# A 2176-token attention and two-MLP kernel: blocks of 384 and 512 tokens become one block of 128 and four of 512, and the block of 128 is multiplied with the operands' roles exchanged

## The chip, the core and the metric

One core of one Trainium2 chip. The metric is device time in microseconds (us), less is better. The kernel before was run three times: median 824.35 us, from 822.9 to 825.61.

## What is computed

The reference, cut to what matters:

```python
# attention over 4 batches x 8 heads, 512 local and 32 global tokens each, head size 64
out_g = softmax(q_g k_all^T / 8) v_all          # global queries see all 544 keys
out_l = softmax([q_l k_g^T, banded(q_l k_l^T)] / 8) [v_g, v_l]   # local: globals and 32 to each side
x = concat(out_g, out_l)                        # 2176 tokens x 512 features
for w_in, w_out in two MLPs:                    # 512 -> 2048 -> 512
    x = relu(x @ w_in) ** 2 @ w_out             # all in fp32 accuracy
```

The weights arrive as 64-bit floats and are narrowed on the chip.

## The kernel before

**Precision.** Each fp32 product of the MLPs is three matmuls in the fast fp32 form: both operands are split into a rounded part ("hi") and a remainder ("lo"), and `three` (L637 to L640) adds hi x hi, hi x lo and lo x hi in one PSUM bank. Whatever is multiplied is split first: ScalarE copies the hi part, VectorE subtracts it to make the lo part (`minus`, L271).

**Blocks.** The 2176 tokens are held with features on the partitions and tokens along the row, in five blocks: 0 (384 tokens, the last 256 local ones and the 128 global ones), 1 and 2 (512 each), 3 and 4 (384 each). Blocks 1 and 2 form pair A, blocks 3 and 4 pair B. In a matmul a 128x128 tile of the weights is the stationary operand and a block's tokens are the moving one, so a matmul of block 0 or pair B moves 384 columns and one of pair A 512.

**Stages.** The hidden layer of 2048 is worked through 256 columns at a time, 8 times in each MLP. The very first of these 16 rounds is the "first wave" (L1096 to L1103): block by block, 48 matmuls for each (24 with `first`, L784, into a bank `h`; 24 with `second`, L733, into banks `Y`). Its block 1 goes in two halves of 256. The other 15 rounds are the stages. In a stage block 0 is still worked with 48 matmuls. A pair is worked by a Winograd scheme of seven products instead of eight: `products` (L815) takes 42 matmuls, and `back` (L936) another 42. Where the table `so` says so, `plain` (L928) takes the place of `back`, with 48 matmuls a stage and less work for VectorE. The table `order` gives the sequence of A, B and 0 in each stage. The last pair of a stage is held, and its `back` is done in the next stage over both stages' products at once, so that its result is added to the running sum `y` once and not twice. Pair A goes plain in one stage's worth (stage 6), pair B in four (stage 0, two at stage 6, one at stage 7).

**What the other engines do in a stage.** For a pair: sums of products (`plus`, L869), ReLU and square (`square`, L896), four differences (`mix`, L953, on VectorE where `gt` says D), seven splits (`op`, L912: ScalarE L922, VectorE L271), fourteen additions to `y` for two stages (`deliver`, L704). For block 0: two squares, two splits, four additions to `y`, which `sd` partly gives to ScalarE as a seed of the bank (L744) and a copy back (L756). The next weights are fetched, narrowed on VectorE (L569 to L575), summed (L588) and split (L598, L271). Before each MLP `tsums` (L998) forms the input sums of both pairs: for each of two halves 8 VectorE operations (4 before the second MLP) and 4 remainders. The second square of ReLU's result goes to ScalarE or VectorE by `gf` (L907, L910).

**The attention** (`pair`, L367, 32 calls, and `glob`, L463, four calls) runs ahead of the stages, and the first wave fills TensorE's gaps in it. `glob` uses the storage of two blocks' `y` for its values (`GLOB_V`), so those blocks' first sums wait until the last `glob` is through (L688). The masks, scores and the identity matrix for transposes lie in a pool of SBUF that is given back when the attention is through; the later weight and operand buffers lie in the same space.

**Order.** Nothing is ordered by hand: each operation is given an engine, an estimated cost, a priority and its dependencies (`Plan.add`), and `Plan.order` simulates the engines and emits the program in that order. The loads go through one queue, SP's. All numbers of `CFG` (priorities such as `moe`, `glob`, `lead`, `w0`; engine choices such as `gt`, `gf`, `sx`, `xh`; buffer counts such as `NS`, `NM`, `GE`) feed that plan, so a change of them moves the order of everything.

Of the kernel before, what the change touches and what calls it, by code (L numbers as in the profile page):

```python
# [38 lines left out]
PAIRW = 1  # L39
CFG = {'warm': 13,  # L40
 'sg': 'A',
 'tl': 'DD',
 'EARLY': 4,
 'vc': 'P',
 'ev': 'AAA',
 'yc': 'AAAA',
 'wl': 'D',
 'gl': 'DD',
 'xh': 'A',
 'glob': [4.59, 16.35, 31.81, 49.0],  # L50
 'w0': 15.637277868928315,
 'w1': 0.6214172823321102,
 'halves': [1],
 'moe': [1605.016, 3061.337, 408.024, 510.431, 1148.554, 4092.57],
 'step': [0.3436, 318.4918, 0.0092, 0.0015, 18.2233, 2.7083],
 'NK': 3,
 'wa': 'AADAAAD',
 'lid': -10.973,
 'lmk': -60.126,
 'lead': 30.668,  # L60
 'vlead': 30.108,
 'NM': 2,
 'NS': 4,
 'NV': 3,
 'NR': 14,
 'NWR': 1,
# [173 lines left out]
def kernel(ctx: ExitStack, tc: tile.TileContext, kl, vl, gk, gv, gr, win, wout, msk, idn, out):  # L240
# [543 lines left out]
    def first(P, W, b, n, f, late, half=None):  # L784

        nb, c0 = (NB[b], 0) if half is None else (256, 256 * half)
        slot = W["in"][n]
        c3 = 3 * pe_r(nb)
        hk = take("h", CFG["h"] + CFG["S"] if late else CFG["h"])
        hp = bank[hk][:, 0:nb]  # L790
        for k in range(KD):
# [4 lines left out]
        if f is None:
            r, R = staging()
            square(P, nb, hp, hk, r[:, 0:nb], R)
            return r[:, 0:nb], R
# [304 lines left out]
    for layer in range(2):  # L1106
        steps = [p for p in range(STAGES) if layer or p >= FW]
        for p in steps:
# [10 lines left out]
            for n, j in enumerate(order):  # L1119
# [136 lines left out]
```

## Time and profile before

| | |
|---|---|
| median of three runs | 824.35 us |
| the profiled execution | 826.18 us |
| its span, first to last instruction | 824.1 us |
| mean granted TensorE clock | 0.990 of full speed |
| TensorE busy | 793.9 us, 6316 matmuls |
| VectorE busy | 702.4 us, 1485 instructions |
| ScalarE busy | 582.0 us, 1184 instructions |
| GpSimd busy | 61.3 us, 132 instructions |
| DMA | 188.99 MB, mean 229 GB/s |

How to read it: the time of an execution is its span and some 2 us around it. Matmuls overlap one another, so a row's duration (0.33 us for 384 columns) is longer than the time from one start to the next (0.17 us), and it is the starts that tell what a matmul costs. The same holds to a lesser degree for VectorE. A busy share is a mean over stretches with different limits; the table of stretches further down tells them apart. The granted clock has two levels here, 2.4 GHz (1.00) and half of it; a value between them is a stretch with both.

### The profile page before, as it was taken

The numbers are of one execution on the slowest core, as the hardware profiler recorded it, in microseconds if no ns is written. First come the engines' busy times: TensorE is split into PE (matmuls) and PEld (weight loads), VectorE is DVE, ScalarE is ACT, GpSimd is POOL, SyncE is SP. The second block draws the span as 40 slices with busy tenths as digits, with TensorE's granted clock in tenths as the row PEclk, the third lists the DMA queues.
The fourth block names the chain that finished last, engine by engine and source line by source line (L and its number), as shares of the span: only waits on it lengthen the run. The fifth ranks groups of instructions, "written<-read, shape, count | busy, mean of one in ns | idle before, by whom it ended". The sixth has DMA issues, their size and how long they took to land.

```text
span 824.1 us, 16763 instructions
## 1 busy us (share of the span) xinstructions
PE 793.9 (96%) x6316; PEld 701.9 (85%) x6316; DVE 702.4 (85%) x1485; ACT 582.0 (71%) x1184; POOL 61.3 (7%) x132
## 2 busy tenths in 40 slices
PE   8898899979999999999999889999999999999998
PEld 5576678978899988998899678889988998899887
DVE  4787767996989988998979996869898998999887
ACT  5795878678747774867677977778684757586853
POOL 2535254000000000000000000000000000000000
PEclk9998999989999999999999999999999999999999
DMA  9986853376729574775464479919674488557723
GB/s 342 349 317 242 305 180 103 124 269 245 281 61 346 202 281 136 258 289 207 151 238 166 166 288 319 355 39 341 247 275 138 146 331 275 181 207 285 265 82 141
DMA packets 74481, 188.99 MB, mean 229 GB/s; under 512 B 7201, under 2 KB 31905, under 8 KB 74401
## 3 DMA queue, kind: packets, MB, share of 16 engines
q1 hardware_dynamic: 74400, 187.92, 64.4%
q8 instruction: 50, 0.82, 0.4%
q14 instruction: 31, 0.25, 0.1%
HBM read 168.23 MB, written 19.66 MB: 228 GB/s over the span
## 4 chain that ended last, share of the span: by engine, by line
PE 81%; DVE 10%; DMA 4%; ACT 2%; issue 2%; SPq 1%; DVEq 0%; ACTq 0%
PE h L638 8%; PE h L640 7%; PE h L639 7%; PE O L640 6%; PE O L639 6%; PE O L638 6%; PE S L640 5%; PE S L639 5%; PE S L638 5%; PE Y L638 3%; PE Y L639 3%; PE Y L640 3%; PE PT L640 3%; PE PT L639 3%; PE PT L638 3%; PE S L393 2%
## 5 line engine op out<-in xcount | busy, mean ns | idle before, releaser
L922 ACT ACTIVATE gh<-r 128x384 fp32r<-128x384 f32 (+1 forms) x225 | 125.8, 569 | 71.3 <-PE PT L640 28.5
L271 DVE TENSOR_TENSOR gl<-r,gh 128x384 fp32r<-128x384 f32 (+2 forms) x237 | 141.2, 611 | 12.3 <-ACT gh L922 11.9
L704 DVE TENSOR_TENSOR y<-y,O 128x384 f32<-128x384 f32 (+1 forms) x115 | 68.3, 614 | 14.4 <-PE O L640 14.3
L640 PE MATMUL O<-gh,wlo 128*128 128x384 f32 (+1 forms) x208 | 74.2, 357 | 0.0
L639 PE MATMUL O<-gl,whi 128*128 128x384 f32 (+1 forms) x208 | 74.2, 357 | 0.0
L638 PE MATMUL O<-gh,whi 128*128 128x384 f32 (+1 forms) x208 | 74.1, 356 | 0.0
L910 ACT ACTIVATE r<-r 128x384 f32<-128x384 f32 (+1 forms) x131 | 72.2, 563 | 1.6
L264 POOL TENSOR_SCALAR v<-v 64x260 f32<-64x260 f32 (+2 forms) x128 | 61.1, 485 | 80.9 <-DMA v<-vl 50.7
L953 DVE TENSOR_TENSOR r<-r,r 128x512 f32<-128x512 f32 (+1 forms) x100 | 61.0, 630 | 2.5 <-ACT r L910 2.3
L271 DVE TENSOR_TENSOR wlo<-wt,whi 128x1024 fp32r<-128x1024 f32 x45 | 55.0, 1222 | 5.2 <-ACT whi L598 5.1
L598 ACT ACTIVATE whi<-wt 128x1024 fp32r<-128x1024 f32 x45 | 47.6, 1057 | 16.2 <-DVE wt L575 8.3
L638 PE MATMUL h<-xh,whi 128*128 128x384 f32 (+2 forms) x146 | 51.9, 356 | 5.7 <-ACT r L905 5.7
L903 ACT ACTIVATE r<-r 128x512 f32<-128x512 f32 (+1 forms) x75 | 43.0, 575 | 17.2 <-DVE r L869 17.1
L638 PE MATMUL h<-tr,whi 128*128 128x512 f32 (+1 forms) x138 | 52.0, 377 | 2.8 <-ACT r L256 1.6
L256 ACT ACTIVATE r<-h 128x512 f32<-128x512 f32 (+1 forms) x65 | 35.5, 546 | 25.6 <-PE h L640 25.3
L407 ACT ACTIVATE s<-s,mn 128x128 f32<-128x128 f32 x128 | 44.4, 397 | 11.4 <-DVE mn L402 10.8
L869 DVE TENSOR_TENSOR r<-r,S 128x384 f32<-128x384 f32 (+1 forms) x64 | 39.6, 623 | 14.2 <-PE S L640 11.6
L639 PE MATMUL h<-tr,whi 128*128 128x512 f32 (+1 forms) x138 | 51.7, 374 | 0.0
L640 PE MATMUL h<-tr,wlo 128*128 128x512 f32 (+1 forms) x138 | 51.6, 374 | 0.0
L588 DVE TENSOR_TENSOR wt<-wt 128x256 f32<-128x256 f32 x120 | 50.5, 421 | 1.2
L639 PE MATMUL h<-xl,whi 128*128 128x384 f32 (+2 forms) x146 | 49.2, 337 | 1.4 <-issue 1.4
L640 PE MATMUL h<-xh,wlo 128*128 128x384 f32 (+2 forms) x146 | 49.3, 338 | 0.7 <-DVE wlo L271 0.7
(174 smaller groups left out, 2234.8 us busy)
## 6 DMA issues: line engine op xcount, KB each, us to landing
tr<-tdA SPq DMA_DIRECT2D x86, 512.0 KB, 4.9
tr<-tdB SPq DMA_DIRECT2D x78, 384.0 KB, 4.5
tr<-xd SPq DMA_DIRECT2D x56, 512.0 KB, 5.1
wraw<-win SPq DMA_DIRECT2D x32, 512.0 KB, 6.1
wraw<-wout SPq DMA_DIRECT2D x32, 512.0 KB, 5.7
kq<-kl SPq DMA_DIRECT2D x32, 352.0 KB, 5.1
v<-vl SPq DMA_DIRECT2D x32, 260.0 KB, 4.8
kg<-gk SPq DMA_DIRECT2D x8, 576.0 KB, 6.8
```

Source lines behind the costliest of these rows:

```text
L264: add("Pool", 0.16 + 0.00085 * n + (0.08 if key == "nm" else 0.0), prio, lambda: nc.gpsimd.tensor_scalar(out=out_, in0=in_, scalar1=1.0 if ...
L271: add("DVE", dve(n), prio, lambda: nc.vector.tensor_tensor(out=get(out_), in0=get(a), in1=get(b), op=ALU.subtract), reads, writes, lock=True)
L407: add("Activation", 0.29, P(), lambda k=k: nc.scalar.activation(out=st[sb][:, k, :], in_=st[sb][:, k, :], func=AF.Exp, bias=mn[sb][:, k:k ...
L588: add("DVE", dve(256), P(), lambda out_=out_, a=a, b=b, op=op: nc.vector.tensor_tensor(out=half(*out_), in0=half(*a), in1=half(*b), op=op) ...
L598: nc.scalar.activation(out=whi[p], in_=tf, func=AF.Copy)
L638: nc.tensor.matmul(out=out_, lhsT=hi, rhs=xhi, start=start, stop=False, skip_group_check=again)
L639: nc.tensor.matmul(out=out_, lhsT=hi, rhs=xlo, start=False, stop=False, skip_group_check=again)
L640: nc.tensor.matmul(out=out_, lhsT=lo, rhs=xhi, start=False, stop=stop, skip_group_check=again)
L704: add("DVE", dve(nb), P(), lambda: nc.vector.tensor_tensor(out=yd, in0=yd, in1=o, op=ALU.add), (k,), (Y,))
L910: add("Activation", act(nb) + 0.04, P(), lambda: nc.scalar.activation(out=r, in_=r, func=AF.Square), (), (R,))
L922: nc.scalar.activation(out=a(), in_=r, func=AF.Copy)
L953: add("DVE", dve(nb), P(), lambda: nc.vector.tensor_tensor(out=o, in0=x, in1=z, op=ALU.subtract), rd, (O,), lock=True)
```

## The change

The blocks become 0 (the 128 global tokens), 1, 2, 3 and 4 (512 each). Pair B now moves 512 columns too. Block 0 no longer goes through `first` and `second`: in `first0` its activations are the stationary operand and the weights of both halves of the 256 hidden columns are the moving one (12 matmuls of 256 columns), so tokens land on the partitions. `second0` transposes the squared result back (2 transposes), splits it and multiplies with it as the stationary operand and 512 weight columns as the moving one (6 matmuls). The sum `y` of block 0 stays transposed, 128 tokens by 512 features, in one addition a stage, and is transposed (4 transposes) at the end of each MLP. In the first wave the last two blocks, 4 and 0, now may use the attention's banks (four in all for each kind); before only the last block did. The identity matrix moves to the lasting pool. `GLOB_V` moves from blocks 4 and 0 to 4 and 3. All of the plan's numbers are set anew; the ones spoken of here are in the diff. By the new tables pair A goes plain in one stage's worth again (6) and pair B in five (0, two at 6, one at 7, and the last, 14).

```diff
-NB = [384, 512, 512, 384, 384]
-OFF = [1792, 0, 512, 1024, 1408]
+NB = [128, 512, 512, 512, 512]
+OFF = [2048, 0, 512, 1024, 1536]
-GLOB0 = 256
-GLOB_V = (4, 0)
+GLOB0 = 0
+GLOB_V = (4, 3)
...
- 'xh': 'A',
- 'glob': [4.59, 16.35, 31.81, 49.0],
- 'w0': 15.637277868928315,
+ 'xh': 'AADD',
+ 'glob': [4.85, 15.36, 30.45, 61.1],
+ 'w0': 19.433405025148332,
...
- 'lead': 30.668,
- 'vlead': 30.108,
- 'NM': 2,
- 'NS': 4,
+ 'lead': 85.79,
+ 'vlead': 230.95,
+ 'NM': 3,
+ 'NS': 7,
...
- 'order': ['B0A', 'A0B', 'B0A', '0AB', 'B0A', '0AB', 'B0A', 'B0A', 'A0B', 'B0A', 'A0B', '0BA', 'A0B', 'B0A', 'AB0'],
+ 'order': ['B0A', 'A0B', 'BA0', 'AB0', 'B0A', '0AB', 'B0A', 'B0A', '0AB', 'BA0', '0AB', 'B0A', 'A0B', '0BA', '0AB'],
- 'gt': 'DDDDDDD',
- 'GE': 21,
- 'so': ['A', 'AB', 'B', 'A', 'AB', 'AB', '', 'A', 'A', 'B', 'AB', 'AB', 'A', 'B', 'AB'],
- 'fk': 'FKF',
- 'sx': 'D',
- 'sd': 'DADAAA',
- 'gf': 'ADAA',
+ 'gt': 'DDDDDPDD',
+ 'GE': 2,
+ 'so': ['A', 'A', 'AB', 'AB', 'B', 'AB', '', '', 'A', 'AB', 'A', 'B', 'AB', 'B', 'A'],
+ 'fk': 'FFF',
+ 'sx': 'AD',
+ 'sd': 'DAAADD',
+ 'gf': 'A',
...
-    ident = ap_.tile([128, 128], F32, name="ident")
+    ident = big.tile([128, 128], F32, name="ident")
...
+    def first0(P, W, late):
+        hk = take("h", CFG["h"] + CFG["S"] if late else CFG["h"])
+        o = bank[hk][:, 0:256].rearrange("p (f c) -> p f c", f=2)
+        for k in range(KD):
+            def go(k=k):
+                a, l = xh[0][:, k, :], xl[0][:, k, :]
+                h, r = both_(whi, W["in"])[:, k], both_(wlo, W["in"])[:, k]
+                nc.tensor.matmul(out=o, lhsT=a, rhs=h, start=k == 0, stop=False)
+                nc.tensor.matmul(out=o, lhsT=l, rhs=h, start=False, stop=False)
+                nc.tensor.matmul(out=o, lhsT=a, rhs=r, start=False, stop=k == KD - 1)
...
+        square(P, 256, bank[hk][:, 0:256], hk, r[:, 0:256], R)
+        return r, R
+    def second0(P, rR, W, stages, late, f=None):
...
+        o, tk = flip(P, r, R, 2, kinds)
...
+        split_in(P, o, tk, 256, hi, lambda: gl[f][:, 0:256], keys("gh", f, None) + lw, keys("gl", f, None), lr)
...
+        for n in range(2):
...
+                nc.tensor.matmul(out=bank[yk], lhsT=a, rhs=whi[p][:, c], start=n == 0, stop=False)
+                nc.tensor.matmul(out=bank[yk], lhsT=l, rhs=whi[p][:, c], start=False, stop=False)
+                nc.tensor.matmul(out=bank[yk], lhsT=a, rhs=wlo[p][:, c], start=False, stop=n == 1)
...
+            add("DVE", dve(512), P(), lambda: nc.vector.tensor_tensor(out=yflat[0], in0=yflat[0], in1=bank[yk], op=ALU.add), (yk,), (Y,))
+        if not end:
+            return
+        o, tk = flip(P, yflat[0], Y, 4, kinds)
...
-        last = i == len(parts) - 1
+        last = i >= len(parts) - 2
+        if b == 0:
+            second0(P, first0(P, W, last), W, (0, True, False), last, 0)
+            continue
...
-                    mine = [first(P, W, 0, i, None, True) for i in range(2)]
+                    mine = first0(P, W, True)
...
-                        second(P, 0, [op(P, NB[0], *v) for v in mine], W["out"], True, True, stages)
+                        second0(P, mine, W, stages, True)
```

## Rows read from the trace of the kernel before

**Rows 1.** Busy time, share, instructions: TensorE, its weight loads, VectorE, ScalarE, GpSimd.

```profile
PE 793.9 (96%) x6316; PEld 701.9 (85%) x6316; DVE 702.4 (85%) x1485; ACT 582.0 (71%) x1184; POOL 61.3 (7%) x132
```

**Rows 2.** Stretches: length, busy PE, PEld, DVE, ACT, POOL, granted clock, DMA, GB/s.

```profile
200.00:440.00 240.00, 240.00 (x1229) 219.85 (x1228) 215.73 (x356) 166.26 (x304) 0.00 (x0) 1.00 0.62 222
260.00:280.00 20.00, 20.00 (x107) 18.70 (x106) 19.73 (x41) 11.71 (x22) 0.00 (x0) 1.00 0.76 274
450.00:500.00 50.00, 43.73 (x208) 37.80 (x207) 49.83 (x85) 41.69 (x81) 0.00 (x0) 0.97 0.65 228
148.00:176.00 28.00, 22.48 (x113) 21.20 (x112) 27.72 (x47) 21.93 (x41) 0.00 (x0) 0.89 0.57 187
0.00:148.00 148.00, 134.45 (x2981) 101.50 (x2982) 105.36 (x491) 108.76 (x321) 61.30 (x132) 0.98 0.74 256
```

**Rows 3.** TensorE in time order, 512 columns: first and thirtieth of a run.

```profile
202.41 0.39 PE L638 MATMUL S<-xh,whi 128*128 128x512 f32 x1
...
208.98 0.39 PE L640 MATMUL PT<-gh,wlo 128*128 128x512 f32 x1
```

**Rows 4.** TensorE in time order, 384 columns: first and seventieth of a run.

```profile
419.99 0.33 PE L638 MATMUL PT<-gh,whi 128*128 128x384 f32 x1
...
431.95 0.33 PE L638 MATMUL O<-gh,xh 128*128 128x384 f32 x1
```

**Rows 5.** TensorE in time order, 256 columns: first and fourth of a run.

```profile
57.04 0.28 PE L640 MATMUL Y<-gh,wlo 128*128 128x256 f32 x1
...
57.40 0.29 PE L640 MATMUL Y<-gh,wlo 128*128 128x256 f32 x1
```

**Rows 6.** TensorE in time order: two transposes among matmuls of 384 columns.

```profile
141.33 0.38 PE L447 MATMUL O<-ident,og 128*128 128x128 f32 x2
141.47 0.42 PE L638 MATMUL h<-xh,whi 128*128 128x384 f32 x1
141.73 0.33 PE L639 MATMUL h<-xl,whi 128*128 128x384 f32 x1
```

**Rows 7.** VectorE in time order, back to back, three widths.

```profile
457.17 0.42 DVE L588 TENSOR_TENSOR wt<-wt 128x256 f32<-128x256 f32 x1
457.51 0.55 DVE L725 TENSOR_TENSOR xl<-y,xh 128x384 fp32r<-128x384 f32 x1
457.98 0.42 DVE L588 TENSOR_TENSOR wt<-wt 128x256 f32<-128x256 f32 x1
...
462.19 0.68 DVE L869 TENSOR_TENSOR r<-r,S 128x512 f32<-128x512 f32 x1
462.78 0.69 DVE L271 TENSOR_TENSOR gl<-r,gh 128x512 fp32r<-128x512 f32 x1
```

**Rows 8.** Differences of the pairs on VectorE, and its share of the squares.

```profile
L953 DVE TENSOR_TENSOR r<-r,r 128x512 f32<-128x512 f32 (+1 forms) x100 | 61.0, 630 | 2.5 <-ACT r L910 2.3
...
L907 DVE SCALAR_TENSOR_TENSOR r<-h,r x14: 550/554/687, 182.0 to 768.5; 128x384 f32<-128x384 f32 x10, 128x512 f32<-128x512 f32 x4
```

**Rows 9.** TensorE in time order: the wait for a transfer at 62 us.

```profile
64.34 1.11 PE L393 MATMUL S<-kq 64*32 64x128 f32 x32 [2.08 <-DMA kq<-kl]
```

**Rows 10.** TensorE in time order: the idle time after the first wave.

```profile
165.51 0.34 PE L640 MATMUL O<-gh,wlo 128*128 128x384 f32 x1
170.95 0.80 PE L638 MATMUL h<-xh,whi 128*128 128x512 f32 x1 [5.09 <-ACT r L905]
```

**Rows 11.** The two stretches with a low granted clock, columns as in rows 2.

```profile
60.00:70.00 10.00, 7.45 (x92) 5.84 (x90) 5.96 (x17) 5.62 (x16) 4.88 (x8) 0.71 0.80 306
170.00:180.00 10.00, 9.05 (x35) 8.77 (x36) 8.92 (x14) 6.71 (x13) 0.00 (x0) 0.66 0.58 193
```

**Rows 12.** GpSimd in time order: four copies of 260 columns.

```profile
140.33 2.12 POOL L264 TENSOR_SCALAR v<-v 128x260 f32<-128x260 f32 x4 [0.50 <-DMA v<-vl]
```

**Rows 13.** VectorE at the same time.

```profile
140.44 0.70 DVE L271 TENSOR_TENSOR xl<-r,xh 128x384 fp32r<-128x384 f32 x1
141.07 0.41 DVE L459 TENSOR_TENSOR xl<-O,xh 128x256 fp32r<-128x256 f32 x1
```

More of the change, by code (lines that the diff above doesn't have):

```diff
@@ L39 @@
 PAIRW = 1
-CFG = {'warm': 13,
- 'sg': 'A',
+SWAP = 1
+CFG = {'warm': 22,
+ 'sg': 'AA',
  'tl': 'DD',
@@ L44 @@
  'vc': 'P',
[L45 to L47 removed]
+ 'ev': 'A',
+ 'yc': 'ADADA',
+ 'wl': 'DDD',
  'gl': 'DD',
[L49 to L52 removed]
+ 'xh': 'AADD',
+ 'glob': [4.85, 15.36, 30.45, 61.1],
+ 'w0': 19.433405025148332,
+ 'w1': 2.6779652430424033e-05,
  'halves': [1],
[L54 to L55 removed]
+ 'moe': [168.634, 2327.744, 1007.075, 700.535, 1092.751, 4389.972],
+ 'step': [0.111, 8.2134, 0.0159, 0.0005, 188.9438, 4.4386],
  'NK': 3,
[L57 to L63 removed]
+ 'wa': 'DADDDDA',
+ 'lid': -57.239,
+ 'lmk': -136.889,
+ 'lead': 85.79,
+ 'vlead': 230.95,
+ 'NM': 3,
+ 'NS': 7,
  'NV': 3,
@@ L77 @@
  'NTR': 6,
- 'gt': 'DDDDDDD',
- 'GE': 21,
- 'tm': 'SRSR',
- 'so': ['A', 'AB', 'B', 'A', 'AB', 'AB', '', 'A', 'A', 'B', 'AB', 'AB', 'A', 'B', 'AB'],
- 'wp': [-276.82, -549.97],
- 'fk': 'FKF',
- 'sf': 'A',
- 'sx': 'D',
- 'ds': 0.267,
- 'ls': 0.051,
- 'sd': 'DADAAA',
- 'yd': 'DD',
- 'NY': 12,
- 'gf': 'ADAA',
- 'gs': 'A',
+ 'gt': 'DDDDDPDD',
+ 'GE': 2,
+ 'tm': 'RRRS',
+ 'so': ['A', 'A', 'AB', 'AB', 'B', 'AB', '', '', 'A', 'AB', 'A', 'B', 'AB', 'B', 'A'],
+ 'wp': [-459.04, -617.67],
+ 'fk': 'FFF',
+ 'sf': 'A',
+ 'sx': 'AD',
+ 'ds': 0.291,
+ 'ls': 0.082,
+ 'sd': 'DAAADD',
+ 'yd': 'DDDD',
+ 'NY': 44,
+ 'gf': 'A',
+ 'gs': 'AA',
  'begin': [1, 2, 3, 4, 0],
@@ L795, in first @@
         wide[hk] = nb
[L796 to L799, printed above, removed]
         activate(P, f, nb, hp, hk, half)
+    both_ = lambda t, slots: t[slots[0] // 2].rearrange("p (f k c) -> p k f c", f=2, k=KD)
+    def first0(P, W, late):
[8 more added lines that the diff above has]
+                nc.tensor.matmul(out=o, lhsT=a, rhs=r, start=False, stop=k == KD - 1)
+            add("PE", 3 * pe_r(256), P(), go, (("w", W["in"][0] // 2), ("x", 0, k)), (hk,))
+        wide[hk] = 256
+        r, R = staging()
+        square(P, 256, bank[hk][:, 0:256], hk, r[:, 0:256], R)
+        return r, R
@@ new lines, in flip, with go, split_in @@
+    def flip(P, src, rd, n, kinds):
+        tk = take("Y", kinds)
+        def go():
+            for i in range(n):
+                nc.tensor.transpose(bank[tk][:, 128 * i:128 * i + 128], src[:, 128 * i:128 * i + 128], ident)
+        add("PE", 0.109 * n, P(), go, (rd, "ident"), (tk,), mode="T")
+        wide[tk] = 0
+        return bank[tk][:, 0:128 * n], tk
+    def split_in(P, o, tk, n, hi, lo, hw, lw, rd=()):
+        add("Activation", act(n), P(), lambda: nc.scalar.activation(out=hi(), in_=o, func=AF.Copy), (tk,) + rd, hw)
+        add("DVE", dve(n), P(), lambda: nc.vector.tensor_tensor(
+            out=lo(), in0=o, in1=hi().bitcast(F32), op=ALU.subtract), (tk,) + hw, lw)
@@ new lines, in second0, with hi, go @@
+    def second0(P, rR, W, stages, late, f=None):
+        layer, begin, end = stages
+        kinds = CFG["Y"] + CFG["PT"] + CFG["O"] if late else CFG["Y"]
+        r, R = rR
+        o, tk = flip(P, r, R, 2, kinds)
+        f = operand() if f is None else f
+        lr, lw = late_keys(("g", f)) if f >= GE else ((), ())
+        def hi():
+            if f >= GE:
+                open_late()
+            return gh[f][:, 0:256]
+        split_in(P, o, tk, 256, hi, lambda: gl[f][:, 0:256], keys("gh", f, None) + lw, keys("gl", f, None), lr)
+        done_with(R)
+        yk = take("Y", kinds)
+        for n in range(2):
+            def go(n=n):
+                a, l = gh[f][:, 128 * n:128 * n + 128], gl[f][:, 128 * n:128 * n + 128]
+                p, c = W["out"][n] // 2, slice(512 * (W["out"][n] % 2), 512 * (W["out"][n] % 2) + 512)
+                nc.tensor.matmul(out=bank[yk], lhsT=a, rhs=whi[p][:, c], start=n == 0, stop=False)
+                nc.tensor.matmul(out=bank[yk], lhsT=l, rhs=whi[p][:, c], start=False, stop=False)
+                nc.tensor.matmul(out=bank[yk], lhsT=a, rhs=wlo[p][:, c], start=False, stop=n == 1)
+            add("PE", 3 * pe_r(512), P(), go, (("w", W["out"][n] // 2),) + keys("gh", f, None) + keys("gl", f, None), (yk,))
+        wide[yk] = 512
+        Y = ("y", 0, 0)
+        if begin:
+            copy("yc", P(), yflat[0], bank[yk], 512, (yk,), (Y,), psum=True)
+        else:
+            add("DVE", dve(512), P(), lambda: nc.vector.tensor_tensor(out=yflat[0], in0=yflat[0], in1=bank[yk], op=ALU.add), (yk,), (Y,))
+        if not end:
+            return
+        o, tk = flip(P, yflat[0], Y, 4, kinds)
+        if layer == 0:
+            X = tuple(("x", 0, k) for k in range(KD))
+            split_in(P, o, tk, 512, lambda: xh[0].rearrange("p k n -> p (k n)"), lambda: xl[0].rearrange("p k n -> p (k n)"), X, X)
+        else:
+            z, Z = staging()
+            copy("yc", P(), z, o, 512, (tk,), (Z,), psum=True)
+            load(P(), out[:, OFF[0]:OFF[0] + 128].rearrange("(k p) c -> p k c", p=128), z.rearrange("p (k c) -> p k c", k=KD), 262144, (Z,), ())
+            done_with(Z)
```

3 lines of the change are left out of this document (1 added, 2 removed).

## The prediction

> **What bounds the kernel now.** First the page's busy shares: TensorE is at 96% [rows 1]. A share of the whole span says little, so next the table of stretches [rows 2]. From 200 to 440 us TensorE is busy for all of 240.00 us, VectorE for 215.73, which is 89.9%, and ScalarE for 166.26. There a matmul less is time less. From 450 to 500 us, between the two MLPs, it is the other way round: VectorE 49.83 of 50, TensorE 43.73. The same at the end of the first wave, from 148 to 176 us: VectorE 27.72 of 28, TensorE 22.48. In the attention, 0 to 148 us, neither is full. So the change must be read in four places: stages, the passage between the MLPs, the start of the stages, the attention.
>
> Last the price of a matmul, from its starts and not from its duration. Thirty matmuls of 512 columns lie 6.57 us apart from first to last, 29 steps of 0.2266 us [rows 3]; seventy of 384 columns 11.96 us, 69 steps of 0.1733 [rows 4]; 256 columns take 0.36 us for 3 steps, 0.120 [rows 5]. Each is its columns at 2.4 GHz plus 13 ns.
>
> **The stages, TensorE.** Before: pair A 84 x 0.2266 = 19.04 us, pair B 84 x 0.1733 = 14.56, block 0 48 x 0.1733 = 8.32, together 41.92. After: both pairs 19.04. Block 0: 12 x 0.120 = 1.44 and 6 x 0.2266 = 1.36, and two transposes. From the start of two transposes to that of the second matmul behind them are 0.40 us, with one matmul of 0.17 among them, so 0.23 for the two and the change of mode [rows 6]. Block 0 costs 3.03, the stage 41.11: 0.81 us less. The 256 columns are priced from matmuls that load a new stationary tile each, as `first0` does, so I see no other price for them.
>
> TensorE sets the time in 13 of the 15 stages; at 6 and 7, around the passage, VectorE does. 13 x 0.81 = **10.5 us less**. Against it: pair B's plain unit at stage 0 is wider, 6 x 0.053 = 0.32; one more plain unit at stage 14 costs 6 x 0.2266 = 1.36; the last flip has 4 transposes, at 0.11 about 0.44 (the one between the MLPs lies in TensorE's idle time). **+2.1 us.** The first wave: before 48 x (2 x 0.120 + 0.2266 + 3 x 0.1733) = 47.2, after 48 x (0.240 + 3 x 0.2266) + 3.0 = 47.1: nothing.
>
> Here a rule says less. In the Trainium skill, "TensorE: Matmul & The Clock Gate", section "Back-to-back issue gap", an isolated warm matmul has a gap of its columns at 2.4 GHz plus 2.5 ns. The trace does not agree (13 ns); by the rule fewer, longer matmuls gain less: an estimate from it is 0.49 us a stage, 6.4 in place of 10.5, and the sum below would end 4 us higher.
>
> **The stages, VectorE.** Back to back it takes 0.34 us for 256 columns, 0.47 for 384, 0.59 for 512 [rows 7]. Pair B has per stage 7 remainders, 4 differences, some 2.5 sums of products and 7 additions to `y`, each 0.12 longer: +2.46. Block 0 had two remainders and, with 4 of 6 additions on ScalarE, 1.33 additions, 1.57 us; it now has one of 256 and one of 512, 0.93: -0.64. The squares leave VectorE: 14 of them in one row [rows 8], 10 x 0.47 + 4 x 0.59 = 7.1 us, -0.47 a stage. The 100 differences become 56 + 40 = 96, of which every eighth, 12, goes to GpSimd: -0.47. `sx` copies one bank into another in half of 12 calls and so saves 12 additions: at most -0.47. In all +0.4. VectorE's 0.899 x 41.92 = 37.7 us become 38.1 of 41.11: 93%. I take TensorE to remain the bound, because VectorE ran at 19.73 of 20 us beside a TensorE at 20.00 [rows 2]; the cover is thin. ScalarE at 69% loses the seeds of block 0 and gains the squares and wider rows, and hides them. The wider transfers of pair B (6 a stage, 128 KB more each) add about 19 GB/s to the 222 GB/s of the stages [rows 2]; the core reached 306 in a stretch of the attention [rows 11], so I cost them at nothing; if the cover goes, SP's queue stands behind them, and the weights with it.
>
> Block 0's chain now passes TensorE twice (product, square, transpose, split, product) with 3 us of its own work where 8.3 stood between a pair's products and its `back`. TensorE lost nothing to such chains from 200 to 440 us, since the plan places other pairs' work in between: nothing at best, and two operations of 0.6 us a stage, 18 us, if never covered. I take nothing.
>
> **The passage between the MLPs.** VectorE sets it, so its work counts whole. Added: 16 `tsums` operations, 6 splits, 12 remainders, 5 sums of pair B, 39 x 0.12 = 4.7; eight plain additions to `y`, of which ScalarE now takes half and not two thirds, +1.1. Removed: block 0 in two stages 1.3, its four splits for one 1.3, two squares 0.9. **+2.3 us.**
>
> **The start.** Two idle times stand there. At 62 us TensorE waits 2.08 us for a transfer of keys [rows 9], and the clock is then at half for a while: 0.71 over 10 us, worth 2.9 [rows 11]. At 165.5 us it waits 5.09 [rows 10], and 0.66 over 10 us is 3.4 more [rows 11]. All of it would be 13.5 us. `lead` and `vlead` move the key and value loads ahead of the others in SP's queue (the weights of the first wave come later by it), and score buffers are seven and not four. On the other side, `tsums` of pair B costs VectorE 24 x 0.12 = 2.9 us in a stretch where it is full; and block 3's first sums must wait for the last `glob`, now at 61.1, with its Y bank and 24 matmuls, 5.4 us, behind them. Nothing in the trace shows the new order, so the bounds are -13.5 and +8.3; the middle is -2.6, and nearest to the one edit that is plain is the wait for keys, about 2.1: I take **-2.4 us**. The further edits (the identity's pool, warm-up matmuls, half of the `xh` copies to VectorE, which has 105.36 of 148 us busy there [rows 2]) are covered by engines that wait.
>
> **The sum.** The profiled execution took 826.18 us, its span 824.1. -10.5 + 2.1 + 2.3 - 2.4 = -8.5: 817.7. It was 1.8 above the median of the runs, so **816 us** against 824.35. A measurement tells some 0.3% from no change, 2.5 us.
>
> **Rivals.** *VectorE becomes the bound.* Over 240 us it never did more than 89.9%. If that is what its waits leave it, 38.1 us of work take 42.4, 0.46 longer than the stage before; 13 x 0.46 = 6.0, and 2.3 at the passage: 832.6, slower. It decides once VectorE's work passes 0.899 x 41.92 = 37.7 us. For it: 38.1 is past that; against it the stretch at 19.73 of 20, and that GpSimd gets 12 differences. That help may be none: while GpSimd ran four copies [rows 12], a VectorE remainder of 384 columns took 0.63 us to the next start, in place of 0.47 [rows 13, 7]. If each difference on GpSimd held VectorE for 1.0 us (twice the columns of those copies, at 0.53 each), VectorE would gain 0.8 us a stage, and this rival would end near 844. The Trainium skill, "SBUF — State Buffer", section "SBUF: two separate sides", says the same as a rule: the port pair that both share is an exclusive lock, and the loser blocks for the whole instruction; the trace agrees in kind, with a loss of 0.16 us.
>
> *The start eats it.* Block 3's second half lands behind the attention: 5.4 + 2.9 lost there, nothing gained: 816 + 2.4 + 8.3 = about 826.5, no change. For it: `glob` at 61.1 of 64. Against it: the attention is itself short of TensorE time, so what leaves it ends it earlier.
>
> *The start pays in full.* -13.5 in place of -2.4: 805. For it: seven score buffers, and block 4 on four banks, so that 19 us of the first wave (24 x 0.2266 for block 3, 48 x 0.2266 or 10.9 for block 4, 3.0 for block 0) cover VectorE's 28 us.
>
> **Chances.** The forecast 0.50 (its own range 811 to 821, faster but for 0.02), VectorE 0.20 (slower 0.17, same 0.03), start eats it 0.13 (0.02 faster, 0.07 same, 0.04 slower), start pays 0.17 (faster). Faster 0.67, same 0.12, slower 0.21. The range of 8 in 10 goes from 804, just below the case that pays in full, to 830: the upper half of VectorE's cases and a tail below are left out.
>
> **What would show it.** Right: starts of 0.227 in both pairs, 0.120 in `first0`; block 0 at 3 us of TensorE a stage; TensorE full in the middle stages, VectorE at 92 to 93%; VectorE full between the MLPs for longer; no wait for keys near 62 us. Wrong: TensorE idle behind remainders or differences in the middle stages (the VectorE rival), remainders of 0.6 us stretched beside GpSimd, or a longer idle time before stage 0 (the start).

## The result and the profile after

The changed kernel takes **816.34 us** (median of 4 runs, 815.62 to 818.58) beside 824.89 for the kernel before in the same comparison: ratio 0.9893, interval 0.9868 to 0.9918. The forecast was 816 with a range from 804 to 830. The profiled execution took 816.24 us, its span is 814.5; that of before took 826.18 and 824.1.

The busy shares of the changed kernel, from the page (TensorE, weight loads, VectorE, ScalarE, GpSimd):

```profile
PE 783.2 (96%) x5900; PEld 631.6 (78%) x5900; DVE 711.3 (87%) x1419; ACT 559.3 (69%) x1047; POOL 75.6 (9%) x144
```

Against [rows 1] the share of TensorE is the same 96% and its busy time is 10.7 us shorter, while VectorE is busy for 8.9 us more. The span went with TensorE.

The same stretches as in [rows 2, 11], in the same columns, of the changed kernel:

```profile
200.00:440.00 240.00, 239.27 (x1088) 198.49 (x1087) 220.94 (x336) 164.58 (x272) 7.37 (x5) 1.00 0.67 248
450.00:500.00 50.00, 46.33 (x204) 36.95 (x203) 49.79 (x80) 39.77 (x70) 0.00 (x0) 0.97 0.72 264
148.00:176.00 28.00, 20.52 (x89) 15.42 (x88) 27.83 (x45) 21.11 (x37) 0.00 (x0) 0.90 0.57 197
170.00:180.00 10.00, 7.14 (x21) 4.93 (x22) 9.96 (x16) 7.46 (x13) 0.00 (x0) 0.66 0.60 212
60.00:70.00 10.00, 7.41 (x174) 5.65 (x169) 8.80 (x40) 7.30 (x23) 4.41 (x8) 1.00 1.01 354
```

In the middle stages VectorE is busy for 220.94 of 240, which is 92.1%, and TensorE for 239.27 beside it. Between the MLPs and at the end of the first wave VectorE is full as before, and the clock behind the first wave is again 0.66. From 60 to 70 us, where it was 0.71, it is 1.00; more on this in the part on the start below.

TensorE of the changed kernel in time order (start, duration, line, operation, idle time before and what ended it): the wait for keys, the end of the first wave, and one stretch of the middle stages:

```profile
68.12 1.16 PE L394 MATMUL S<-kq 64*32 64x128 f32 x32 [1.02 <-DMA kq<-kl]
...
163.07 0.38 PE L827 MATMUL Y<-ident,r 128*128 128x128 f32 x2
163.92 0.50 PE L860 MATMUL PT<-whi,gh 128*128 128x512 f32 x1 [0.47 <-ACT gh L835]
165.68 0.50 PE L861 MATMUL PT<-whi,gl 128*128 128x512 f32 x1 [1.25 <-DVE gl L836]
...
166.71 0.40 PE L862 MATMUL PT<-wlo,gh 128*128 128x512 f32 x1
172.34 0.80 PE L639 MATMUL h<-xh,whi 128*128 128x512 f32 x1 [5.24 <-ACT xh L1107]
...
282.94 0.28 PE L811 MATMUL S<-whi,xh 128*128 128x256 f32 x1
283.06 0.28 PE L812 MATMUL S<-whi,xl 128*128 128x256 f32 x1
283.17 0.28 PE L813 MATMUL S<-wlo,xh 128*128 128x256 f32 x1
283.29 0.40 PE L639 MATMUL h<-tr,whi 128*128 128x512 f32 x1
...
286.73 0.38 PE L827 MATMUL O<-ident,r 128*128 128x128 f32 x2
286.86 0.47 PE L639 MATMUL h<-tr,whi 128*128 128x512 f32 x1
287.17 0.39 PE L640 MATMUL h<-tr,whi 128*128 128x512 f32 x1
...
290.16 0.39 PE L641 MATMUL h<-tr,wlo 128*128 128x512 f32 x1
296.74 0.39 PE L640 MATMUL h<-tr,whi 128*128 128x512 f32 x1
```

The three matmuls of block 0 take 0.35 us to the next start, 0.117 each; two transposes and a matmul 0.44, so 0.21 for the transposes; the last two lines are 29 steps apart, 0.227 each. The wait for keys [rows 9] is 1.02 us instead of 2.08. The idle time before the stages [rows 10] is 5.24 instead of 5.09, so it did not go.

**Where the time went.** Three points can be found in every trace: the first matmul behind that idle time (called the start of the stages here; by the count of matmuls 30 of stage 0 stand ahead of it in both kernels), the last start of the four splits of `y` for block 1 (the end of the first MLP), and the last matmul. The splits, as groups of one line, before and then after, with first and last start:

```profile
L725 DVE TENSOR_TENSOR tr<-y,tr x4: 686/686/690, 468.0 to 475.8; 128x512 fp32r<-128x512 f32 x4
```

```profile
L726 DVE TENSOR_TENSOR tr<-y,tr x4: 685/686/689, 464.6 to 472.4; 128x512 fp32r<-128x512 f32 x4
```

The last matmul, before and then after, in TensorE's time order:

```profile
820.25 0.34 PE L640 MATMUL O<-gh,wlo 128*128 128x384 f32 x1
```

```profile
810.09 0.39 PE L641 MATMUL PT<-gh,xl 128*128 128x512 f32 x1
```

| | start of the stages | to the end of the first MLP | to the last matmul | to the end of the span |
|---|---|---|---|---|
| before | 170.95 | 304.85 | 344.45 | 3.85 |
| after | 172.34 | 300.06 | 337.69 | 4.41 |
| difference | +1.4 | -4.8 | -6.8 | +0.6 |

The two MLPs together went from 649.3 to 637.75 us, 11.55 less. Between those two matmuls the program before has 1266 matmuls of 512 columns and 1974 of 384, at 0.2266 and 0.1733 that is 629.0 us; the program after has 2628 of 512, 168 of 256 and 38 transposes, at 0.2266, 0.120 and 0.115 that is 620.0. So **8.9 us are matmul time**, and 2.6 are less waiting. Most of that stands at the passage between the MLPs, before and then after, in the columns of [rows 2]:

```profile
440.00:520.00 80.00, 73.18 (x353) 63.86 (x352) 69.64 (x117) 64.20 (x120) 0.00 (x0) 0.98 0.73 257
```

```profile
440.00:520.00 80.00, 75.41 (x338) 60.46 (x337) 71.37 (x110) 60.88 (x106) 0.00 (x0) 0.98 0.74 269
```

TensorE is idle for 6.82 us before and 4.59 after, although VectorE is busy for 1.7 us more. With 20 us more on the right, 440 to 540, it is 6.82 and 5.46, since a wait of the changed kernel falls just behind the window; so the passage gives 1.4 to 2.2 us.

### The profile page after: what moved, and what is told of

It reads as the page before. It is cut to its first block, busy times and chain, and to the rows that moved or that the text cites. A ratio compares the mean times of both kernels' runs of the same rounds, so it can differ in the third digit from the quotient of the medians.

```text
span 814.5 us, 15728 instructions
## 1 busy us (share of the span) xinstructions
PE 783.2 (96%) x5900; PEld 631.6 (78%) x5900; DVE 711.3 (87%) x1419; ACT 559.3 (69%) x1047; POOL 75.6 (9%) x144
## 4 chain that ended last, share of the span: by engine, by line
PE 87%; DVE 6%; DMA 3%; ACT 2%; issue 1%; POOL 0%; ACTq 0%
PE h L639 6%; PE O L640 6%; PE h L640 6%; PE O L641 6%; PE h L641 6%; PE O L639 6%; PE S L639 6%; PE S L640 5%; PE S L641 5%; PE Y L639 4%; PE Y L641 4%; PE Y L640 4%; PE PT L640 3%; PE PT L641 3%; PE PT L639 3%; PE O L430 2%
## 5 line engine op out<-in xcount | busy, mean ns | idle before, releaser
L1001 ACT ACTIVATE gh<-r 128x512 fp32r<-128x512 f32 x192 | 118.6, 628 | 77.9 <-DVE r L1032 26.6
L272 DVE TENSOR_TENSOR gl<-r,gh 128x512 fp32r<-128x512 f32 (+1 forms) x202 | 135.6, 689 | 11.4 <-ACT gh L1001 10.9
L640 PE MATMUL O<-gl,whi 128*128 128x512 f32 x168 | 66.4, 395 | 0.1
L639 PE MATMUL O<-gh,whi 128*128 128x512 f32 x168 | 66.4, 395 | 0.0
L641 PE MATMUL O<-gh,wlo 128*128 128x512 f32 x168 | 66.1, 394 | 0.0
L705 DVE TENSOR_TENSOR y<-y,O 128x512 f32<-128x512 f32 x80 | 53.4, 681 | 8.5 <-PE O L641 8.5
L1032 DVE TENSOR_TENSOR r<-r,r 128x512 f32<-128x512 f32 x84 | 58.1, 708 | 1.8 <-ACT r L989 1.5
L589 DVE TENSOR_TENSOR wt<-wt 128x256 f32<-128x256 f32 x120 | 51.0, 425 | 1.7
L639 PE MATMUL Y<-gh,whi 128*128 128x512 f32 (+1 forms) x121 | 47.5, 392 | 1.5 <-ACT y L257 1.5
L982 ACT ACTIVATE r<-r 128x512 f32<-128x512 f32 x60 | 37.4, 624 | 12.2 <-DVE r L948 12.1
L641 PE MATMUL Y<-gh,wlo 128*128 128x512 f32 (+1 forms) x121 | 45.5, 376 | 0.2 <-DVE wlo L272 0.2
L574 DVE SCALAR_TENSOR_TENSOR wt<-wraw,wt 128x1024 uint32<-128x1024 uint32 x32 | 39.3, 1228 | 0.5
L576 DVE SCALAR_TENSOR_TENSOR wt<-wraw,wt 128x1024 uint32<-128x1024 uint32 x32 | 39.4, 1231 | 0.1
```

What stands on the lines that cost most here:

```text
L272: add("DVE", dve(n), prio, lambda: nc.vector.tensor_tensor(out=get(out_), in0=get(a), in1=get(b), op=ALU.subtract), reads, writes, lock=True)
L589: add("DVE", dve(256), P(), lambda out_=out_, a=a, b=b, op=op: nc.vector.tensor_tensor(out=half(*out_), in0=half(*a), in1=half(*b), op=op) ...
L639: nc.tensor.matmul(out=out_, lhsT=hi, rhs=xhi, start=start, stop=False, skip_group_check=again)
L640: nc.tensor.matmul(out=out_, lhsT=hi, rhs=xlo, start=False, stop=False, skip_group_check=again)
L641: nc.tensor.matmul(out=out_, lhsT=lo, rhs=xhi, start=False, stop=stop, skip_group_check=again)
L705: add("DVE", dve(nb), P(), lambda: nc.vector.tensor_tensor(out=yd, in0=yd, in1=o, op=ALU.add), (k,), (Y,))
```

## The experiments

The open questions were: is the gain the new block sizes with block 0's exchange of operands, or the new numbers of the plan; how near is VectorE to being the bound, and does GpSimd help it; and what holds the start of the stages. The program's order is written by a planner from costs and due times, so most edits change the whole order. This turned out to matter more than the edits, and the last four runs were made with it in view. The kernel before drifted between the comparisons (median 824.80 in that of e1 to e4, 826.11 for e5 to e8, 828.03 for f1 to f4), so runs are compared by their ratios to it, or by the stretches of the table above.

### The blocks and the numbers

**e3: the old blocks with the new numbers.** The kernel before with the new `CFG` and four banks:

```diff
-CFG = {'warm': 13,
- 'sg': 'A',
+CFG = {'warm': 22,
+ 'sg': 'AA',
...
- 'NM': 2,
- 'NS': 4,
...
+ 'NM': 3,
+ 'NS': 7,
...
```

> The kernel before with all of the change's new plan numbers and its four banks, but the old blocks and no exchange. Theory (the gain is TensorE's 0.81 us a stage): 824 less what the new numbers give by themselves at the start, 820 to 827. Rival (the new numbers are the gain): 816.

832.4 us, ratio 1.0095 (1.0068 to 1.0122). Both forecasts on record missed: the numbers alone are no gain, they make the old blocks slower.

**e2: the new blocks without the exchange.** Block 0 goes through the matmuls of before (each stationary tile is weights or tokens as there, 128 columns wide), with the new sizes, numbers and banks:

```diff
-    def first0(P, W, late):
...
+        if f is None:
+            r, R = staging()
+            square(P, nb, hp, hk, r[:, 0:nb], R)
+            return r[:, 0:nb], R
```

> The blocks of the change (128 and four of 512) and its numbers, but block 0 goes through first and second as before, 48 matmuls of 128 columns a stage. Theory: if 128 columns cost their columns plus 13 ns (0.067 us), block 0 takes 3.2 us a stage against 3.03 and the time is 816 + 13 x 0.2 = about 819; if loading the stationary tile sets the start, and 128 columns cost as much as 256 (0.120), it takes 5.8 and the time is 816 + 13 x 2.7 = about 851. Either way the exchange of roles is what the second case makes worth having. Rival (the block's size does it, not the exchange): 816.

871.56 us, ratio 1.0562 (1.0528 to 1.0595). TensorE in time order, block 0 in the middle stages:

```profile
301.79 0.28 PE L639 MATMUL O<-gl,whi 128*128 128x128 f32 x1
301.90 0.27 PE L640 MATMUL O<-gh,wlo 128*128 128x128 f32 x1
302.01 0.27 PE L638 MATMUL O<-gh,whi 128*128 128x128 f32 x1
302.12 0.27 PE L639 MATMUL O<-gl,whi 128*128 128x128 f32 x1
```

A matmul of 128 columns starts 0.11 us after the one before: almost what 256 columns cost. Forty-eight of them are 5.3 us a stage against 3.0 with the exchange; 15 x 2.3 is 34 us. Against e1 below, which also runs in an order that was not made for it, e2 is 35 us slower. The higher number on record, 851, had the price of the matmuls nearly right and the order at nothing; the time lies 20 above it, as e1 lies 20 above 816. So the exchange carries the small block; without it, sizes of 128 and 512 lose to 384 and 512.

**e4: block 0's first product twice.**

```diff
-        for k in range(KD):
+        for k in list(range(KD)) * 2:
```

> The changed kernel with the 12 matmuls of first0 issued twice, the second time over the first (same result): 12 x 0.120 = 1.44 us of TensorE more in each of 15 stages and the first wave. Theory (TensorE sets 13 of 15 stages): +18.7, so 835; the two stages around the passage hide theirs. Rival (VectorE sets the time already): under +8, because the added matmuls fill TensorE's waits.

841.29 us, ratio 1.0219 (1.0175 to 1.0263). Its end of the first MLP and its last matmul:

```profile
L726 DVE TENSOR_TENSOR tr<-y,tr x4: 683/683/684, 478.9 to 485.9; 128x512 fp32r<-128x512 f32 x4
```

```profile
835.60 0.39 PE L641 MATMUL PT<-gh,xl 128*128 128x512 f32 x1
```

With its stages beginning at 175.15, the first MLP is 10.7 us longer than in the changed kernel and the second 12.0, together 22.7. Between the two marks its trace has 336 matmuls of 256 columns and the changed kernel's 168 (14 stages' worth, stage 0's lie ahead of the start), and 168 x 0.12 are 20.2 us. So TensorE's time counts in full in the sum, and more than the 835 on record, which left two stages out. But the plan was told of the added matmuls and made a new order, and a new order alone cost 20 us in e1. That this one cost next to nothing is not shown, nor which stages paid; the agreement may be luck in part.

### The order

**e1: two numbers of the plan.** Only what the planner believes of two latencies:

```diff
- 'ds': 0.291,
- 'ls': 0.082,
+ 'ds': 0.267,
+ 'ls': 0.051,
```

> The changed kernel with the plan's two latency numbers (ds, ls) as in the kernel before: no instruction is added or removed, only the order written by the plan moves. Theory (TensorE's work sets the time, the order little): 816, within 2.5 us. Rival (the 8.5 us are a lucky order): the time moves by 5 us or more. This also says how far any other run here must move before its edit may be named as the cause.

836.17 us, ratio 1.0135 (1.0095 to 1.0176). The same work in another order costs 20 us, twice the gain of the change. The theory on record for this run fell.

**e7: the new code with all of before's numbers.**

```diff
-CFG = {'warm': 22,
- 'sg': 'AA',
+CFG = {'warm': 13,
+ 'sg': 'A',
...
```

> The change's blocks and exchange with every plan number of the kernel before (order, so, engine choices, buffers, priorities), four banks kept. Theory (TensorE's columns are the gain): 816 plus 0.5 of VectorE work a stage that is hidden, less one plain unit of pair B fewer (1.4), with a worse start; 813 to 822. Rival (the numbers are the gain): 822 to 830.

850.14 us, ratio 1.0282 (1.0249 to 1.0314): by the ratios 32 us lost, the most of any plan tried here, and far from both ranges on record.

**e8 and f3: `lead` and `vlead` alone**, taken back in the changed kernel (e8) and put into the kernel before (f3):

```diff
- 'lead': 85.79,
- 'vlead': 230.95,
+ 'lead': 30.668,
+ 'vlead': 30.108,
```

> The changed kernel with lead and vlead as before (30.7 and 30.1), so the key and value loads stand later in SP's queue. Theory (the start gained nothing by them: the first matmul of the stages begins at 172.34 us and at 170.95 before): no change, 814 to 819. Rival (the loads ahead hold the start together): 2.4 us or more slower, with the wait for keys near 62 us of 2 us and the half clock behind it.

> The kernel before with lead and vlead of the change, an edit of the attention's loads alone, the counterpart of e8_old_lead. Theory (any new order costs the tuned kernel some 8 to 12 us, of the old blocks as of the new): 830 to 837, most of the loss long after the attention. Rival (the old blocks' time does not hang on the order, and the change's gain is one of its order only): 824, within 2.5 us. A third case (the leads are themselves a gain): 822.

e8: 828.21 us, ratio 1.0019 (1.0001 to 1.0037). f3, the same diff turned round in the code of before: 832.57, 1.0049 (1.003 to 1.0067). So these two numbers are worth 10 us to the new blocks and cost the old ones 4 (the time of f3 lies in the range on record, but the loss is half of the 8 to 12 it was to come from). But they do not pay where they act: e8 has no wait for keys near 62 us, and its clock is 1.00 from 60 to 70 us. In e8 the stages begin 1.0 us later than in the changed kernel, the first MLP is 1.5 longer, and 9.7 us are lost behind it. A stretch of the second MLP, changed kernel and then e8:

```profile
520.00:800.00 280.00, 278.64 (x1264) 230.09 (x1263) 253.80 (x390) 189.09 (x310) 10.18 (x7) 1.00 0.65 243
```

```profile
520.00:800.00 280.00, 274.38 (x1231) 223.21 (x1232) 250.90 (x381) 184.55 (x303) 10.59 (x7) 1.00 0.66 245
```

That is 400 us after the last key was loaded (its load is issued at 117.5 us). TensorE's order in e8 is the changed kernel's from 22 to 477 us, but for 12 matmuls at 180 us, and again from 720 us on; between 477 and 720 the planner placed the matmuls otherwise, and there the 9.7 us are lost.

**Like with like.** The gain of the new blocks can be read from pairs of kernels that stand alike towards their numbers, from the first matmul of the stages to the last. Each with the numbers it came with: 649.3 us for the old blocks, 637.75 for the new, -11.6. Each with the other's `lead` and `vlead`: 655.6 (f3) and 648.95 (e8), -6.7. Each in an order not made for it: 654.1 (e3) and 646.5 (e1), -7.6, or -5.5, as the stretch of e3 has 12 matmuls of stage 0 (2.1 us) that lie ahead of the start elsewhere. The new blocks are shorter by 5 to 12 us in these three pairs; the count of matmuls says 8.9. Each stretch is of one execution (e1's took 4.6 us less than its median). A fourth pair goes the other way: each with the other's whole set of numbers, the new blocks take 850.14 us (e7) and the old ones 832.4 (e3), by the ratios 15 us more. So the gain is not one that the blocks have under any numbers: the old ones lose 8 us by the new numbers, the new ones 32 by the old.

### VectorE and GpSimd

**e5 and f1: more work for VectorE.** e5 issues one remainder in some of the operands again (46 operations more) and lets the plan be made anew; f1 issues every fourth remainder of 512 columns twice (57 more in the trace, 1476 against 1419) with the order kept:

```diff
+        if f % 4 == 0:
+            minus("gl", P(), l, r, lambda: a().bitcast(F32), nb, (R,) + GH, GL)
```

```diff
+            picks["m"] = picks.get("m", 0) + (n == 512); times = 2 if n == 512 and picks["m"] % 4 == 0 else 1
...
```

> The changed kernel with every fourth operand's remainder computed twice (same result): some 3.5 more VectorE operations of 512 columns a stage, 3.5 x 0.59 = 2.1 us. Theory (TensorE sets the stages, VectorE has 41.1 - 38.1 = 3.0 us of room a stage): 816 plus what falls in the two VectorE-bound stretches, 2 x 2.1 = 4, so about 820. Rival (VectorE's 92% is already its ceiling): 13 x 2.1 / 0.92 = +30 and 4 at the stretches, so about 850.

> The changed kernel in its own order on every engine; every fourth remainder of 512 columns (of operands and of tsums, some 54) is computed twice in its place, with the plan not told of it: 54 x 0.59 = 32 us of VectorE, 2.1 a stage. Theory (TensorE sets the stages, VectorE has 3.0 us of room a stage, and the 13 us of the run before with a dose were the new order): the doses in the two VectorE-bound stretches count, some 16 x 0.6 = 9, so 816 + 9 = 825, and TensorE stays full from 200 to 440 us. Rival (VectorE's 92% is its ceiling): all 32 us count, 848.

e5: 829.33 us, 1.0047 (1.0029 to 1.0066), between the numbers on record. Its 13 us cannot be told from those of a new order, which alone cost 20 in e1. f1: 839.12, 1.013 (1.0098 to 1.0162). Of its 57 operations 53 lie between the start of the stages and the last matmul, 53 x 0.59 = 31.3 us; that stretch is 21.9 us longer (659.6 against 637.75), so 9.4 us found room, 0.6 a stage. Both numbers on record missed: it is neither free nor fully paid. The middle stages of f1:

```profile
200.00:440.00 240.00, 236.98 (x1058) 191.65 (x1057) 225.77 (x342) 162.28 (x265) 8.52 (x5) 1.00 0.66 246
```

VectorE reaches 94.1%, so neither 89.9% nor 92.1% was a ceiling. And TensorE looks busy for 236.98 of 240 with 30 matmuls fewer than the changed kernel has there. Thirty times 0.2266 is 6.8 us lost, of which only 2.3 show as added idle time (3.02 against 0.73): a matmul's record is 0.39 us long and the next starts 0.23 later, so a short wait disappears under the record before it.

**e6 and f2: GpSimd's 12 differences to VectorE.** e6 by the plan's own letter, and so in a new order; f2 with the order kept:

```diff
- 'gt': 'DDDDDPDD',
+ 'gt': 'DDDDDDDD',
```

```diff
-                add("Pool", 0.25 + 0.0021 * nb, P(), lambda: nc.gpsimd.tensor_tensor(out=o, in0=x, in1=z, op=ALU.subtract), rd, (O,))
+                add("Pool", 0.25 + 0.0021 * nb, P(), lambda: nc.vector.tensor_tensor(out=o, in0=x, in1=z, op=ALU.subtract), rd, (O,))
```

> The changed kernel with all 96 differences on VectorE: 12 x 0.59 = 7 us of VectorE more in all, 0.5 a stage, and nothing on GpSimd after the attention. Theory (room on VectorE): no change, 814 to 819. Rival (a difference on GpSimd holds VectorE longer than doing it itself): faster, by up to 12 x 0.9 = 11 us if VectorE sets the time.

> The changed kernel in its own order; the 12 differences of GpSimd are done by VectorE, at the place that the order gave them. Theory (VectorE has room, and the +16.5 us of the run with a new order came from that order): 814 to 819. Rival (GpSimd's help is worth 16 us): 826 or more. Second rival (a difference on GpSimd holds VectorE): 812 or less.

e6: 832.88 us, 1.0077 (1.005 to 1.0104), outside both ranges on record. f2: 818.41, 0.9878 (0.9839 to 0.9916), the changed kernel's own ratio. The same edit costs 15 us or nothing, by the order it runs in. GpSimd's help is worth nothing that can be measured, and does no harm either.

The changed kernel's trace shows why it is worth so little. GpSimd and then VectorE, at two of the 12 differences:

```profile
227.76 1.58 POOL L1034 TENSOR_TENSOR r<-r,r 128x512 f32<-128x512 f32 x1 [93.75 <-DVE r L1032]
...
399.07 1.62 POOL L1034 TENSOR_TENSOR r<-r,r 128x512 f32<-128x512 f32 x1 [50.96 <-ACT gh L1001]
```

```profile
228.10 1.78 DVE L1032 TENSOR_TENSOR r<-r,r 128x512 f32<-128x512 f32 x1
229.81 0.68 DVE L272 TENSOR_TENSOR gl<-r,gh 128x512 fp32r<-128x512 f32 x1
...
399.44 1.28 DVE L705 TENSOR_TENSOR y<-y,O 128x512 f32<-128x512 f32 x2
400.64 0.68 DVE L948 TENSOR_TENSOR r<-r,h 128x512 f32<-128x512 f32 x1
```

The VectorE difference that starts beside GpSimd's takes 1.71 us to the next start instead of 0.60; the two additions that read a PSUM bank (`O`) take 0.60 each as ever. So it is at all 12: eight VectorE operations with both inputs in SBUF are stretched, by 0.2 to 1.1 us, and none that reads a bank. VectorE loses 4.4 us by it, out of the 12 x 0.59 = 7.1 that it is spared.

### The start of the stages

**f4: less VectorE work ahead of the stages.** For two of the weight conversions the narrowing (L570 to L576) and the sums of L589 are left out, 16 operations and 9.7 us of VectorE, with the order kept; what rests on those weights is then computed from unconverted data.

```diff
-        conv[0] += 1
+        conv[0] += 1; conv_skip = conv[0] in (3, 4)
...
-        add("DVE", dve(1024, True), P(), lambda: nc.vector.tensor_scalar(
+        add("DVE", dve(1024, True), P(), lambda: conv_skip or nc.vector.tensor_scalar(
```

> The changed kernel in its own order, with VectorE's narrowing and sums of stage 0's weights left out (16 operations, 2 x (3.5 + 1.3) = 9.7 us of VectorE between 140 and 185 us; the outputs are wrong by it). Theory (VectorE sets the start of the stages): the idle time of 5.24 us before the first matmul of the stages goes, and with it the half clock behind it, 5 to 9 us: 807 to 811. Rival (ScalarE or a transfer sets it): 816, with the idle time still there.

816.08 us, 0.9856 (0.9824 to 0.9887), the rival's number. TensorE's first matmul of the stages, and VectorE in time order shortly before:

```profile
169.41 0.79 PE L639 MATMUL h<-xh,whi 128*128 128x512 f32 x1 [4.09 <-ACT xh L1107]
```

```profile
159.75 0.69 DVE L260 COPY y<-Y 128x512 f32<-128x512 f32 x1 [2.06 <-PE Y L641]
...
162.07 0.69 DVE L272 TENSOR_TENSOR r<-r,r 128x512 fp32r<-128x512 f32 x1 [1.64 <-PE Y L827]
```

Not all of the 9.7 us lies between 140 and 185 us, as was expected: in the changed kernel the first of the two narrowings, 3.5 us, runs at 63 to 68 us, in the attention, so 6.2 us are taken from ahead of the stages. Of them 2.9 arrive at the start (the stages of f1 and f2, in the same order, begin 1.3 and 0.7 us earlier than the changed kernel's too, so in part this is scatter), and about 1 at the last matmul. VectorE, full until then, now waits 2.06 and 1.64 us for TensorE's sums, and TensorE then waits 4.09 for what VectorE and ScalarE make of them. Each waits for the other in the written order; that VectorE alone held the start fell for the most part.

## Why the prediction was right, and where it was not

**TensorE's stages: right in the prices and the mechanism, with luck in the net.** Every price held: 0.227 for 512 columns, 0.117 for the 256 of `first0`, 0.21 (not 0.23) for two transposes. The net of -8.4 (-10.5 + 2.1) is -8.9 in the count of matmuls, but by other terms. The count has all 15 stages, 15 x 0.81 = 12.2; the prediction set two aside as VectorE's, though TensorE's waits at the passage did not grow. Against them stand all of pair B's plain units (30 matmuls of 512 columns for 24 of 384, 2.6 us where 1.7 were counted) and both flips of four transposes (0.9 where 0.44 were). The differences all but cancel. (The first wave before adds up to 47.4 us and not 47.2, which changes nothing.) In the Trainium skill, "TensorE: Matmul & The Clock Gate", section "Back-to-back issue gap", the gap of an isolated warm matmul is its columns at 2.4 GHz plus 2.5 ns; here, in a stream of matmuls, 512 columns step 0.227 us, 14 ns over their time at 2.4 GHz, so the trace does not agree. In the stages block 0's chain and the wider transfers cost nothing that shows: TensorE waits for 0.73 us of 240 in the middle stages, and all that is not matmul time between the start of the stages and the last matmul fell from 20.3 to 17.7 us. At the end of the first wave the chain does show (below).

**VectorE: right in size, wrong in the room.** 93% forecast, 92.1% measured, with TensorE the bound beside it. The rival at 832.6 rested on 89.9% as a ceiling; f1 went to 94.1%. But the room that the sum implies (38.1 of 41.11, 3.0 us a stage) is not free room: f1 found 0.6 a stage in the order as it stood. VectorE is a near bound, and the order decides how near. The GpSimd rival (844) had the mechanism and not the size: it priced what a difference on GpSimd costs VectorE at 1.0 us, and the trace shows 4.4 / 12 = 0.37, so that f2 moved nothing. The differences on GpSimd took longer than its columns suggested; the group on the changed kernel's page (line, operation, count, then busy us, mean ns, idle us):

```profile
L1034 POOL TENSOR_TENSOR r<-r,r 128x512 f32<-128x512 f32 x12 | 17.5, 1462 | 632.5 <-DVE r L1032 422.4
```

**The passage: wrong, by 4 to 5 us.** "VectorE sets it, so its work counts whole" gave +2.3. VectorE does show more work (71.37 against 69.64 of 80 us), but TensorE's idle time there shrank by 1.4 to 2.2 us, and the stretch in which VectorE is full did not grow. Its first row, and the first row behind its end, each with the idle time ahead of it, before and then after:

```profile
440.87 1.22 DVE L271 TENSOR_TENSOR wlo<-wt,whi 128x1024 fp32r<-128x1024 f32 x1 [0.66 <-ACT whi L598]
...
508.44 0.69 DVE L869 TENSOR_TENSOR r<-r,S 128x512 f32<-128x512 f32 x1 [4.76 <-PE S L640]
```

```profile
441.73 0.69 DVE L726 TENSOR_TENSOR xl<-y,xh 128x512 fp32r<-128x512 f32 x1 [1.34 <-ACT xh L724]
...
507.41 0.69 DVE L272 TENSOR_TENSOR gl<-r,gh 128x512 fp32r<-128x512 f32 x1 [4.61 <-ACT gh L1001]
```

From 440.9 to 503.7 and from 441.7 to 502.8 VectorE never waits for more than 0.2 us: 62.8 us before and 61.1 after. VectorE at 49.8 of 50 us showed that it was full, and neither how long it stays so nor that TensorE had nothing to do meanwhile: the order can put more matmuls beside the same VectorE work. What in the order does it was not tried.

**The start: wrong, by 2 to 4 us.** -2.4 was taken, +1.4 measured; f1 and f2, in the same order, begin their stages at 171.04 and 171.67, which is +0.1 and +0.7. The forecast took the wait for keys as the gain because it was the nearest row, and named the leads. In this execution the wait went from 2.08 to 1.02 us, and the clock is 1.00 from 60 to 70 us where it was 0.71 [rows 11]. But that is this execution and not the order: the clock is 0.83 there in f1, f2 and f4, and in the changed kernel it is low at another place, 10 to 20 us, where the kernel before has 1.00 (before, then after, in the columns of [rows 2]):

```profile
10.00:20.00 10.00, 8.28 (x217) 5.16 (x215) 7.26 (x45) 6.70 (x20) 1.15 (x3) 1.00 1.03 398
```

```profile
10.00:20.00 10.00, 8.28 (x184) 4.62 (x191) 5.84 (x35) 4.58 (x15) 0.00 (x0) 0.84 1.03 400
```

And e8, with the leads taken back, has no such wait either, so the leads are not shown to be what shortens it. The attention does end earlier; its last transposes, before and then after:

```profile
147.76 0.38 PE L447 MATMUL O<-ident,og 128*128 128x128 f32 x2
```

```profile
146.52 0.38 PE L448 MATMUL O<-ident,og 128*128 128x128 f32 x2
```

These 1.2 us are lost again behind it: the last matmul ahead of the idle time starts 1.2 us later (166.71 against 165.51 in [rows 10]), and the idle time is 0.15 longer. Two terms stand there. Block 0's chain was taken at nothing, since other work covers it in the stages; at the end of the first wave TensorE has no other work beside it. From the two transposes at 163.07 to the end of the six matmuls 3.87 us go by for 0.21 + 1.36 = 1.57 us of matmul time, with waits of 0.47 for ScalarE and 1.25 for VectorE; f1, f2 and f4 show the same waits, 0.47 and 0.94 to 1.32. That they move the start is not shown, for VectorE is full behind them and TensorE then waits 5.24 us for its sums and ScalarE's copies of them. The other term is that work of VectorE: the prediction named it (2.9 us more for `tsums` of pair B) and let it into the bound alone. In f4 2.9 of 6.2 us taken from VectorE there arrived; an estimate by that rate is 1.4 us for the 2.9. Of the two rivals, "the start eats it" (8.3 lost) and "the start pays in full" (13.5 gained), neither came.

**The edits costed at nothing: wrong in kind, though it does not show in the sum.** The numbers of the plan were counted as covered by engines that wait, and in detail they are. As a whole they are the order, and the order is worth more than the change: two latencies cost 20 us (e1), two leads 10 (e8), one letter 15 (e6), all numbers 32 (e7). The sum of the matmuls is only had in an order made for them, which the numbers of the change give and nothing in the profile of before could show. And two of the errors above, some -5 at the passage and +4 at the start, cancel in the sum. That the forecast came within 0.4 us of the measured median is luck; the 8.9 us of matmul time are what it had right.

**Left open.** Two banks instead of four for the last blocks, and block 3's sums at their old place, were not tried in a kept order; nor was another order for the passage, or more TensorE work in a kept order. No version here beat the changed kernel by more than the intervals; f2 and f4 are level with it.

## What to carry to other kernels

Where TensorE is full, count its matmuls by columns at the measured step, and mind that a narrow one costs more than its columns: here a block of 128 tokens paid only as the stationary side of the products. A chain between engines that costs nothing in the middle of the work can show at its edges, where no other work stands beside it. Where an order is planned, test an edit with the order kept, or compare pairs that were planned alike; a plan made anew can cost more than the edit. And count the matmuls of a stretch as well as their busy time, since short waits hide under overlapping records.

## What was not expected of the hardware

- A matmul of 128 columns steps 0.11 us in this form, one of 256 columns 0.117 to 0.120, of 384 0.173 and of 512 0.227: a matmul of 128 columns costs almost what one of 256 does (e2).
- A GpSimd difference of 128x512 takes 1.46 us where VectorE takes 0.59 to the next start, and moving twelve of them changed nothing (f2): while GpSimd ran them, VectorE operations with both inputs in SBUF took up to 1.71 us instead of 0.60, and those that read a PSUM bank 0.60 as ever.
- VectorE was busy for 94.1% of 240 us beside a TensorE that did 97% of its matmuls (f1, 1058 of 1088): the room between the two is a matter of a few per cent, not a ceiling.
